# Four PSUM banks as four tiles in the output phase, and a reordered setup, in a fused convolution and GELU feed-forward kernel

## Chip, cores and metric

The kernel runs on one core of one Trainium2 chip. The metric is the device time of one launch in microseconds (us), and the time of a kernel is the median of its runs. The profile is one execution of the same program, taken by the hardware profiler.

## What is computed

A softmax over the 7 taps of 8 heads gives the weights of a causal convolution along the sequence; its result goes through a feed-forward block with the quick GELU. The two weight matrices of that block arrive as float64, and the program rounds them on the chip.

```python
x: (8, 4096, 192)  weight: (8, 7)  w_in: (192, 2048)  w_out: (2048, 192)   # w_in, w_out float64
w = softmax(weight)                       # per head, 24 channels each
c[b, s, d] = sum_k w[head(d), k] * x_pad[b, s + k, d]     # 6 zeros ahead of the sequence
h = c.reshape(32768, 192) @ w_in
g = h * sigmoid(1.702 * h)
out = g @ w_out                           # (32768, 192), float32
```

## The kernel before

The work is cut into 64 steps of 256 positions for each half of the batch. Two neighbouring steps share one load of `x`, one transposition and one convolution: `prepare(big)` yields, for such a pair, three transposes on VectorE (DVE), the load of the next pair, and 21 convolution operations (3 channel groups of 7 taps) that write the tile `ct`. They are spread over the two steps ahead. Each step has two phases on TensorE (PE):

- `hidden(s, u)`, eight times (`u` from 0 to 7): 12 products (float32, so 24 matmul instructions) into a `ph` tile of two banks, out of two that rotate; then ScalarE (ACT) applies the GELU into `g`. A step has 192 matmul instructions of this kind, at line L286.
- `output(s)`: seven products `p1, p6, c11, p7, p5, p3, p4` of a Strassen-Winograd scheme, 96 matmul instructions each (48 at L316 and 48 at L326), into the `po` tile. After each product DVE reads the result out of PSUM: L347 copies it, L350, L355, L358, L360, L362 and L365 add it to a running sum in `u`, and `turn` (L340) transposes a finished quarter into `osb`, which 24 DMAs of the SP queue then write out.

The order of the phases on PE is hidden(0), hidden(1), output(0), hidden(2), output(1), and so on up to hidden(63), output(62), output(63). Between the DVE operations of `output(s-1)` stand the four operations of `sums_g(s)` (L300 to L303), which form the sums of `g` that the products need.

All seven products share one tile of four banks: `p1` and `c11` use bank 0, `p6` and `p3` bank 1, `p7` and `p4` bank 2, `p5` bank 3.

```python
psum_o = ctx.enter_context(tc.tile_pool(name="psum_o", bufs=1, space=bass.MemoryType.PSUM))
po = psum_o.tile([P, NR, TOK], F32, name="po")      # NR = 4 banks
dst = po[:, bank, at : at + TA]
```

Each engine runs its instructions in the order in which the program text emits them; a tile library inserts the waits between engines. In the setup the order is written out by hand: `load_x(0)`, then eight DMAs for four pieces of `w_in` into a scratch area, `prepare(0)` (DVE: transposes and the whole convolution of the first pair), then `round_w_in(0)` (DVE: seven operations over 128x768 and two more over 64x768, then two copies on ACT). hidden(0) follows, with `round_w_in(1)` to `(3)` between its parts and `prepare(1)` spread over steps 0 and 1. After hidden(1) stand `round_w_out(0)` to `(3)` and `sums_w_out`. The scratch area for the raw weights is one of the two buffers of `g`; `g` of step 1 takes the same buffer, so that its first GELU waits until the last `round_w_out` has read it.

Of the kernel before, what the change touches and what calls it, by code (L numbers as in the profile page):

```python
# [8 lines left out]
F32 = mybir.dt.float32  # L9
# [6 lines left out]
def kernel(  # L16
# [56 lines left out]
    u_pool = ctx.enter_context(tc.tile_pool(name="u", bufs=1))  # L73
    osb_pool = ctx.enter_context(tc.tile_pool(name="osb", bufs=2))
    psum_h = ctx.enter_context(tc.tile_pool(name="psum_h", bufs=2, space=bass.MemoryType.PSUM))
    psum_o = ctx.enter_context(tc.tile_pool(name="psum_o", bufs=1, space=bass.MemoryType.PSUM))

    ctx.enter_context(tc.manual_schedule())

# [38 lines left out]

    w8 = consts.tile([H, K], F32)
    nc.scalar.dma_start(out=w8, in_=weight)  # L120
    load_x(0)

    w_in_s = consts.tile([P, NC, F], F32)
    w_in_v = moe_w_in.bitcast(U32).rearrange("(c q) (h f) -> h q c f", q=R, h=2)
    w_out_v = moe_w_out.bitcast(U32).rearrange("(c p) d -> p c d", p=P)

    for i in range(NW):
        piece = raw[:, i, :].rearrange("p (c f) -> p c f", c=NC)  # L130
        cols = slice(2 * i * FW, 2 * (i + 1) * FW)
        for h in range(2):
            nc.sync.dma_start(out=piece[halves[h], :, :], in_=w_in_v[h, :, :, cols])

# [22 lines left out]
    def round_piece(i, dsts):  # L157

        words = raw[:, i, :].rearrange("p (n w) -> p n w", w=2)
        lo, hi = words[:, :, 0], words[:, :, 1]  # L160
        m_hi, m_lo, e, m = (tmp[:, j, :] for j in range(4))
        vec = nc.vector

        vec.tensor_scalar(m_hi, hi, 0xFFFFF, 1 << 20, op0=ALU.bitwise_and, op1=ALU.bitwise_or)
# [11 lines left out]
        for rows, c, cols, dst in dsts:  # L176
            vec.scalar_tensor_tensor(
                out=dst,
                in0=m[rows, :].bitcast(F32).rearrange("p (c n) -> p c n", c=c)[:, :, cols],
                scalar=2.0**-20,  # L180
                in1=e[rows, :].bitcast(F32).rearrange("p (c n) -> p c n", c=c)[:, :, cols],
                op0=ALU.mult,
                op1=ALU.mult,
            )

    def round_w_in(i):
        cols = [slice(h * HF + i * FW, h * HF + (i + 1) * FW) for h in range(2)]
        round_piece(
            i, [(halves[h], NC, slice(0, FW), w_in_s[halves[h], :, cols[h]]) for h in range(2)]
        )  # L190
        for h in range(2):
            nc.scalar.copy(w_in_s[halves[1 - h], :, cols[h]], w_in_s[halves[h], :, cols[h]])

    def load_w_out():
        for i in range(NW):
# [5 lines left out]
    def round_w_out(i):  # L201
        k, j = divmod(i * CW, NK)
        round_piece(
            i,
            [
                (slice(0, P), CW, slice(m * HD, (m + 1) * HD), w_out_s[:, 2 * m + k, j : j + CW, :])
                for m in range(2)
            ],
        )
# [17 lines left out]
    NR = 4  # L227
    pw = psum_o.tile([P, NR, TOK], F32, name="po")[:, 0, 0 : NC * K].rearrange(
        "p (c k) -> p c k", c=NC
    )  # L230
    for c in range(NC):
        nc.tensor.matmul(pw[:, c, :], sel[:, c, :], e8, start=True, stop=True)
    cw = consts.tile([P, NC, K], F32)
# [14 lines left out]
        if c == NC - 1:  # L248
            xins.pop(big)

    def conv(big, i):
        c, k = divmod(i, K)
        if i == 0:
            cts[big] = ct_pool.tile([P, NC, TOK], F32, name="ct")
        src = xts[big][:, c, k : k + TOK]
        dst = cts[big][:, c, :]
        tap = cw[:, c, k : k + 1]
        if k == 0:
            nc.vector.tensor_scalar_mul(dst, src, tap)  # L259
        else:  # L260
            nc.vector.scalar_tensor_tensor(  # L261
                out=dst, in0=src, scalar=tap, in1=dst, op0=ALU.mult, op1=ALU.add
            )

    def prepare(big):

        for c in range(NC):
            yield lambda c=c: transpose_x(big, c)
        if big + 1 < N_BIG:
            yield lambda: load_x(big + 1)  # L270
        for i in range(NC * K):
            yield lambda i=i: conv(big, i)

    def hidden(s, u):

        i, k = divmod(u, 2)
        if u == 0:
            gs[s] = new_g()
        ph = psum_h.tile([P, 2, 2, T], F32, name="ph")
        ct = cts[s // 2]  # L280
        t = s % 2 * T
        for j in range(2):
            f = k * HF + (2 * i + j) * P
            for c in range(NC):
                for h in range(2):
                    nc.tensor.matmul(  # L286
                        ph[:, h, j, :],
                        w_in_s[halves[h], c, f : f + P],
                        ct[halves[h], c, t : t + T],
                        start=(c == 0),  # L290
                        stop=(c == NC - 1),
                    )
        nc.scalar.activation(  # L293
            gs[s][:, 2 * k : 2 * k + 2, 2 * i : 2 * i + 2, :], ph, AF.Gelu_apprx_sigmoid
        )

    def sums_g(s):

        g = [gs[s][:, i, :, :] for i in range(NS)]
        yield nc.vector.tensor_sub(g[T1], g[B12], g[B11])  # L300
        yield nc.vector.tensor_sub(g[T3], g[B22], g[B12])  # L301
        yield nc.vector.tensor_sub(g[T2], g[B22], g[T1])  # L302
        yield nc.vector.tensor_sub(g[T4], g[T2], g[B21])  # L303

    def output(s, others):

        g = gs.pop(s)
        po = psum_o.tile([P, NR, TOK], F32, name="po")
        u = u_pool.tile([P, 4, TA], F32, name="u")
        osb = osb_pool.tile([P, 2, 2, TA], F32, name="osb")  # L310

        def product(a, b, bank, at, first=True):
            dst = po[:, bank, at : at + TA]
            for j in range(NK):
                for c in range(3):
                    nc.tensor.matmul(  # L316
                        dst[c * Q : (c + 1) * Q, :],
                        w_out_s[:, a, j, c * Q : (c + 1) * Q],
                        g[:, b, j, 0:TA],
                        start=(first and j == 0),  # L320
                        stop=(j == NK - 1),
                        skip_group_check=True,
                    )

                for c in range(3):
                    nc.tensor.matmul(  # L326
                        dst[3 * Q :, c * TB : (c + 1) * TB],
                        w_out_s[:, a, j, c * Q : (c + 1) * Q],
                        g[:, b, j, TA:T],
                        start=(first and j == 0 and c == 0),  # L330
                        stop=(j == NK - 1),
                        skip_group_check=True,
                    )
            return dst
# [49 lines left out]
                        ),  # L384
                    )

    for work in prepare(0):
        work()
    round_w_in(0)

    todo = []
    for s in range(N_ST + 1):
        if s < N_ST:
            if s % 2 == 0 and s // 2 + 1 < N_BIG:
                todo = list(prepare(s // 2 + 1))
            n = -(-len(todo) // (2 - s % 2))
            now, todo = todo[:n], todo[n:]
            for u in range(NK):
# [5 lines left out]
                for work in now[u * n // NK : (u + 1) * n // NK]:  # L404
                    work()
            if s == 1:
                for i in range(NW):
                    round_w_out(i)
                sums_w_out()
        others = sums_g(s) if s < N_ST else iter(())  # L410
        if s > 0:
            output(s - 1, others)
        for _ in others:
            pass


# [28 lines left out]
```

## Time and profile before

| | |
|---|---|
| median of 3 runs | 2938.97 us (2938.91 to 2939.54) |
| the profiled execution | 2938.98 us, span 2937.3 us, mean granted clock 0.992 |
| PE busy | 2637.6 us (90% of the span), 55302 matmul instructions |
| DVE busy | 1396.2 us (48%) |
| ACT busy | 533.6 us (18%) |
| POOL (GpSimd) busy | 2.2 us, 11 instructions |
| chain that ended last | PE 89%, DVE 8%, issue 1%, DMA 1% |

Matmuls overlap one another, so a busy PE says that at least one is in flight. What tells more here is the start of the same line in two neighbouring steps, and the rows that name what ended an idle time of PE. Two times of the profile are always given together: when something started, counted from the start of the span, and how long it took.

### The profile page before, as it was taken

What the parts mean: (1) busy time and instruction counts of PE and PEld (TensorE: products, weight loads), DVE (VectorE), ACT (ScalarE), POOL (GpSimd) and SP (SyncE); (2) the same over time, 40 slices, a digit from 0 to 9 for tenths busy, and PEclk for the clock granted to TensorE, in tenths of its full rate; (3) what the DMA queues carried; (4) which work ended last, traced back from release to release, by engine and by line L of the source; (5) the groups of instructions that cost most, each with busy time, mean ns of one, the idle gap of its engine ahead of it and who ended that gap; (6) DMA issues with size and microseconds to landing.
All of it is one profiled execution on the core that took longest, in us unless ns stands there. A gap on an engine that the chain in (4) does not pass through costs nothing.

```text
span 2937.3 us, 115577 instructions
## 1 busy us (share of the span) xinstructions
PE 2637.6 (90%) x55302; PEld 2411.5 (82%) x55302; DVE 1396.2 (48%) x1841; ACT 533.6 (18%) x524; POOL 2.2 (0%) x11
## 2 busy tenths in 40 slices
PE   4599999999999999999999999999999999999997
PEld 3488888888888888888888888888888888888886
DVE  8644445445445444445444444444454454454432
ACT  2121121121121121221211211211211211211210
POOL 0000000000000000000000000000000000000000
PEclk9799999999999999999999999999999999999999
DMA  6011110111110111110111111111101111101000
GB/s 140 3 30 31 27 30 14 27 30 31 28 29 13 28 30 29 30 30 11 29 30 28 29 24 17 30 31 27 29 18 23 30 31 28 30 12 28 12 12 15
DMA packets 293030, 80.90 MB, mean 28 GB/s; under 512 B 223440, under 2 KB 291024, under 8 KB 292560
## 3 DMA queue, kind: packets, MB, share of 16 engines
q1 hardware_dynamic: 292544, 73.51, 14.6%
q8 instruction: 432, 7.08, 1.0%
q14 instruction: 38, 0.31, 0.0%
q10 hardware_dynamic: 16, 0.00, 0.0%
HBM read 48.23 MB, written 25.17 MB: 25 GB/s over the span
## 4 chain that ended last, share of the span: by engine, by line
PE 89%; DVE 8%; issue 1%; DMA 1%; SPq 0%; ACT 0%; ACTq 0%
PE ph L286 46%; PE po L326 26%; PE po L316 18%; DVE osb L340 2%; DVE u L362 1%; DVE u L355 1%; DVE u L358 1%; DVE u L347 1%; DVE u L350 1%; DVE u L360 1%; DMA xin<-in_x_dram 0%; DMA g<-in_moe_w_in_dram 0%; DVE ct L261 0%; ACT g L293 0%; DVE g L173 0%
## 5 line engine op out<-in xcount | busy, mean ns | idle before, releaser
L316 PE MATMUL po<-g,w_out_s 128*32 128x192 f32 x21504 | 1254.8, 328 | 215.9 <-DVE u L360 70.3
L286 PE MATMUL ph<-ct,w_in_s 64*128 64x256 f32 x12288 | 1351.4, 378 | 67.7 <-ACT g L293 35.4
L286 PEld LDWEIGHTS ph<-ct,w_in_s 64*128 64x128 f32 x12288 | 1189.0, 188 | 210.7 <-ACT g L293 35.8
L326 PE MATMUL po<-g,w_out_s 128*32 128x64 f32 x21504 | 1284.6, 220 | 0.0
L326 PEld LDWEIGHTS po<-g,w_out_s 128*32 128x32 f32 x21504 | 1212.2, 110 | 0.0
L316 PEld LDWEIGHTS po<-g,w_out_s 128*32 128x32 f32 x21504 | 834.7, 109 | 299.0 <-DVE u L360 80.6
L293 ACT ACTIVATE g<-ph 128x1024 f32<-128x1024 f32 x512 | 524.0, 1024 | 2314.6 <-PE ph L286 2250.5
L300 DVE TENSOR_TENSOR g<-g 128x2048 f32<-128x2048 f32 x64 | 146.7, 2292 | 659.7 <-ACT g L293 659.7
L261 DVE SCALAR_TENSOR_TENSOR ct<-xt,cw,ct 128x512 f32<-128x512 f32 x576 | 431.8, 750 | 19.4
L303 DVE TENSOR_TENSOR g<-g 128x2048 f32<-128x2048 f32 x64 | 146.2, 2285 | 0.0
L302 DVE TENSOR_TENSOR g<-g 128x2048 f32<-128x2048 f32 x64 | 146.2, 2285 | 0.0
L301 DVE TENSOR_TENSOR g<-g 128x2048 f32<-128x2048 f32 x64 | 146.0, 2281 | 0.3 <-ACT g L293 0.3
L362 DVE TENSOR_TENSOR u<-u,po 128x192 f32<-128x192 f32 x64 | 22.7, 355 | 190.7 <-PE po L326 190.7
L355 DVE TENSOR_TENSOR u<-u,po 128x192 f32<-128x192 f32 x64 | 22.6, 354 | 190.8 <-PE po L326 190.8
L365 DVE TENSOR_TENSOR u<-u,po 128x192 f32<-128x192 f32 x64 | 22.7, 354 | 164.3 <-PE po L326 164.3
L347 DVE COPY u<-po 128x192 f32<-128x192 f32 x64 | 22.9, 358 | 131.7 <-PE po L326 131.7
L340 DVE STREAM_TRANSPOSE osb<-u 128x192 f32<-128x192 f32 x192 | 72.6, 378 | 6.6
L244 DVE STREAM_TRANSPOSE xt<-xin 128x512 f32<-128x512 f32 x96 | 60.3, 679 | 3.5 <-DMA xin<-in_x_dram 3.5
L340 DVE STREAM_TRANSPOSE osb<-po 128x192 f32<-128x192 f32 x64 | 24.5, 382 | 52.0 <-PE po L326 49.1
L350 DVE TENSOR_TENSOR u<-u,po 128x192 f32<-128x192 f32 x64 | 22.7, 354 | 52.3 <-PE po L326 52.3
L358 DVE TENSOR_TENSOR u<-u,po 128x192 f32<-128x192 f32 x64 | 22.6, 353 | 52.0 <-PE po L326 52.0
L259 DVE TENSOR_SCALAR ct<-xt,cw 128x512 f32<-128x512 f32 x96 | 45.1, 470 | 0.0
(34 smaller groups left out, 93.1 us busy)
## 6 DMA issues: line engine op xcount, KB each, us to landing
xin<-in_x_dram SPq DMA_DIRECT2D x128, 320.0 KB, 6.2
out_dram<-osb SPq DMA_DIRECT2D x768, 24.0 KB, 1.6
out_dram<-osb SPq DMA_DIRECT2D x768, 8.0 KB, 1.5
g<-in_moe_w_in_dram SPq DMA_DIRECT2D x8, 384.0 KB, 13.2
g<-in_moe_w_out_dram SPq DMA_DIRECT2D x4, 768.0 KB, 11.5
w<-in_weight_dram ACTq DMA_DIRECT2D x1, 0.2 KB
```

The source lines that it names most:

```text
L244: nc.vector.transpose(xts[big][:, c, PAD:].rearrange("p (j t) -> p j t", t=Q), xins[big][:, :, c * R : c * R + Q],)
L261: nc.vector.scalar_tensor_tensor(out=dst, in0=src, scalar=tap, in1=dst, op0=ALU.mult, op1=ALU.add)
L286: nc.tensor.matmul(ph[:, h, j, :], w_in_s[halves[h], c, f : f + P], ct[halves[h], c, t : t + T], start=(c == 0), stop=(c == NC - 1),)
L293: nc.scalar.activation(gs[s][:, 2 * k : 2 * k + 2, 2 * i : 2 * i + 2, :], ph, AF.Gelu_apprx_sigmoid)
L300: yield nc.vector.tensor_sub(g[T1], g[B12], g[B11])
L301: yield nc.vector.tensor_sub(g[T3], g[B22], g[B12])
L302: yield nc.vector.tensor_sub(g[T2], g[B22], g[T1])
L303: yield nc.vector.tensor_sub(g[T4], g[T2], g[B21])
L316: nc.tensor.matmul(dst[c * Q : (c + 1) * Q, :], w_out_s[:, a, j, c * Q : (c + 1) * Q], g[:, b, j, 0:TA], start=(first and j == 0), stop=(j ...
L326: nc.tensor.matmul(dst[3 * Q :, c * TB : (c + 1) * TB], w_out_s[:, a, j, c * Q : (c + 1) * Q], g[:, b, j, TA:T], start=(first and j == 0 a ...
L340: vec.transpose(osb[:, m, n, :].rearrange("p (j d) -> p j d", d=Q), src.rearrange("p (j t) -> p j t", t=Q),)
L347: vec.tensor_copy(u1, p1)
```

## The change

There are four edits. First, the output phase allocates four `po` tiles of one bank each, from a pool of four buffers, in place of one tile of four banks; the products write the same banks in the same order. Second, the setup is emitted in another order: the first piece of `w_in` is loaded ahead of `x` and rounded ahead of `prepare(0)`, the convolution of the first pair is done in two halves of 256 positions, the first ahead of hidden(0) and the second at its end, the rounding of `w_out` is emitted within hidden(1), and `prepare(1)` as a whole after output(0). Third, `w_in_s` has another layout, so that the last operation of a rounding is one over 128 partitions in place of two over 64. Fourth, the sums of `g` of steps 0 and 1 are on GpSimd.

```diff
-    psum_o = ctx.enter_context(tc.tile_pool(name="psum_o", bufs=1, space=bass.MemoryType.PSUM))
+    psum_o = ctx.enter_context(tc.tile_pool(name="psum_o", bufs=4, space=bass.MemoryType.PSUM))
...
-    load_x(0)
-    w_in_s = consts.tile([P, NC, F], F32)
+    w_in_s = consts.tile([P, NC, 2, HF], F32)
...
             nc.sync.dma_start(out=piece[halves[h], :, :], in_=w_in_v[h, :, :, cols])
+        if i == 0:
+            load_x(0)
...
     def round_w_in(i):
-        cols = [slice(h * HF + i * FW, h * HF + (i + 1) * FW) for h in range(2)]
-        round_piece(
-            i, [(halves[h], NC, slice(0, FW), w_in_s[halves[h], :, cols[h]]) for h in range(2)]
-        )
+        cols = slice(i * FW, (i + 1) * FW)
+        round_piece(i, [(NC, slice(0, FW), w_in_s[:, :, 0, cols])])
         for h in range(2):
-            nc.scalar.copy(w_in_s[halves[1 - h], :, cols[h]], w_in_s[halves[h], :, cols[h]])
+            nc.scalar.copy(w_in_s[halves[1 - h], :, 1, cols], w_in_s[halves[h], :, 0, cols])
...
+        parts = [(0, TOK)] if big else [(0, T), (T, TOK)]
+        for t0, t1 in parts:
+            for i in range(NC * K):
+                yield lambda i=i, t0=t0, t1=t1: conv(big, i, t0, t1)
...
     def sums_g(s):
+        eng = nc.gpsimd if s < 2 else nc.vector
-        yield nc.vector.tensor_sub(g[T1], g[B12], g[B11])
+        yield eng.tensor_sub(g[T1], g[B12], g[B11])
...
-        po = psum_o.tile([P, NR, TOK], F32, name="po")
+        banks = [psum_o.tile([P, TOK], F32, name="po") for _ in range(4)]
...
-            dst = po[:, bank, at : at + TA]
+            dst = banks[bank][:, at : at + TA]
...
-    for work in prepare(0):
+    round_w_in(0)
+    todo = list(prepare(0))
+    for work in todo[: -NC * K]:
         work()
-    round_w_in(0)
+    first = todo[-NC * K :]
...
             for u in range(NK):
                 hidden(s, u)
...
                 if s == 0 and u == NK - 1:
                     load_w_out()
+                    for work in first:
+                        work()
+                if s == 1 and u < NW:
+                    round_w_out(u)
+                    if u == NW - 1:
+                        sums_w_out()
...
         if s > 0:
             output(s - 1, others)
         for _ in others:
             pass
+        if s == 1:
+            for work in todo:
+                work()
```

What the change moves is seen best in the order of the instructions on the engines. On PE, in the output phase of step 4, before, at the end of `c11` and the start of `p7` (the number behind `po` tells tiles apart; DVE_49 is the semaphore that DVE counts up):

```order
L316 MATMUL po_2534<-g_1898,w_out_s_101 32x192 x3
L326 MATMUL po_2534<-g_1898,w_out_s_101 32x64 x3
L316 MATMUL po_2534<-g_1898,w_out_s_101 32x192 [waits DVE_49]
L316 MATMUL po_2534<-g_1898,w_out_s_101 32x192 x2
L326 MATMUL po_2534<-g_1898,w_out_s_101 32x64 x3
```

Every one of the seven products starts with such a wait. The same output phase now, from the end of `p6` (po_2564) over `c11` (po_2563), `p7` (po_2565) and `p5` (po_2566) to `p3`:

```order
L327 MATMUL po_2564<-g_1924,w_out_s_101 32x64 x3
L317 MATMUL po_2563<-g_1924,w_out_s_101 32x192 [waits DVE_49]
L317 MATMUL po_2563<-g_1924,w_out_s_101 32x192 x2
L327 MATMUL po_2563<-g_1924,w_out_s_101 32x64 x3
...
L317 MATMUL po_2565<-g_1924,w_out_s_101 32x192 x3
L327 MATMUL po_2565<-g_1924,w_out_s_101 32x64 x3
...
L317 MATMUL po_2566<-g_1924,w_out_s_101 32x192 x3
L327 MATMUL po_2566<-g_1924,w_out_s_101 32x64 x3
...
L317 MATMUL po_2564<-g_1924,w_out_s_101 32x192 [waits DVE_49]
```

`p1`, `p7` and `p5` have lost their wait. `p6`, `c11`, `p3` and `p4` keep one, now for the last reader of their own bank.

On DVE, at the start of the program, before:

```order
L234 COPY cw<-po 128x21
L240 MEMSET xt 128x3x6
L244 STREAM_TRANSPOSE xt<-xin 128x512 x3
L259 TENSOR_SCALAR ct<-xt,cw 128x512
L261 SCALAR_TENSOR_TENSOR ct<-xt,cw,ct 128x512 x6
...
L164 TENSOR_SCALAR g<-g 128x768
...
L173 SCALAR_TENSOR_TENSOR g<-g 128x768
L177 SCALAR_TENSOR_TENSOR w_in_s<-g 64x3x256 x2
```

and now:

```order
L230 COPY cw<-po 128x21
L165 TENSOR_SCALAR g<-g 128x768
...
L174 SCALAR_TENSOR_TENSOR g<-g 128x768
L178 SCALAR_TENSOR_TENSOR w_in_s<-g 128x3x256
L236 MEMSET xt 128x3x6
L240 STREAM_TRANSPOSE xt<-xin 128x512 x3
L255 TENSOR_SCALAR ct<-xt,cw 128x256
L257 SCALAR_TENSOR_TENSOR ct<-xt,cw,ct 128x256 x6
```

The rounding of the first piece of `w_in` has moved ahead of the transposes, and the convolution ahead of hidden(0) covers half as many positions.

On DVE, around output(0), before, from the last of the four sums of `w_out` on:

```order
L216 TENSOR_TENSOR w_out_s<-w_out_s 128x768
L300 TENSOR_TENSOR g<-g 128x2048
L347 COPY u<-po 128x192
L301 TENSOR_TENSOR g<-g 128x2048
L350 TENSOR_TENSOR u<-u,po 128x192
```

and now, from the same place to the convolution of the second pair:

```order
L215 TENSOR_TENSOR w_out_s<-w_out_s 128x768
L348 COPY u<-po 128x192
L351 TENSOR_TENSOR u<-u,po 128x192
...
L366 TENSOR_TENSOR u<-u,po 128x192
L341 STREAM_TRANSPOSE osb<-u 128x192
L238 COPY xt<-xt 128x3x6
L240 STREAM_TRANSPOSE xt<-xin 128x512 x3
L255 TENSOR_SCALAR ct<-xt,cw 128x512
L257 SCALAR_TENSOR_TENSOR ct<-xt,cw,ct 128x512 x6
```

The sums of `g` have left this place for GpSimd, where the eight operations now stand alone, and the transposes and the convolution of the second pair, which DVE did in steps 0 and 1 ahead of the rounding of `w_out`, have come in behind output(0).

More of the change, by code (lines that the diff above doesn't have):

```diff
@@ L175, in round_piece @@
         )
-        for rows, c, cols, dst in dsts:
+        for c, cols, dst in dsts:
             vec.scalar_tensor_tensor(
                 out=dst,
-                in0=m[rows, :].bitcast(F32).rearrange("p (c n) -> p c n", c=c)[:, :, cols],
+                in0=m.bitcast(F32).rearrange("p (c n) -> p c n", c=c)[:, :, cols],
                 scalar=2.0**-20,
-                in1=e[rows, :].bitcast(F32).rearrange("p (c n) -> p c n", c=c)[:, :, cols],
+                in1=e.bitcast(F32).rearrange("p (c n) -> p c n", c=c)[:, :, cols],
                 op0=ALU.mult,
@@ L205, in round_w_out @@
             [
-                (slice(0, P), CW, slice(m * HD, (m + 1) * HD), w_out_s[:, 2 * m + k, j : j + CW, :])
+                (CW, slice(m * HD, (m + 1) * HD), w_out_s[:, 2 * m + k, j : j + CW, :])
                 for m in range(2)
@@ L226 @@
     nc.vector.tensor_scalar_mul(e8, e8, esum)
[L227 to L230, printed above, removed]
+    pw = psum_o.tile([P, TOK], F32, name="po")[:, 0 : NC * K].rearrange("p (c k) -> p c k", c=NC)
     for c in range(NC):
@@ L249, in transpose_x, with conv @@
             xins.pop(big)
-    def conv(big, i):
+    def conv(big, i, t0=0, t1=TOK):
         c, k = divmod(i, K)
-        if i == 0:
+        if i == 0 and t0 == 0:
             cts[big] = ct_pool.tile([P, NC, TOK], F32, name="ct")
-        src = xts[big][:, c, k : k + TOK]
-        dst = cts[big][:, c, :]
+        src = xts[big][:, c, k + t0 : k + t1]
+        dst = cts[big][:, c, t0:t1]
         tap = cw[:, c, k : k + 1]
@@ L270, in prepare @@
             yield lambda: load_x(big + 1)
-        for i in range(NC * K):
-            yield lambda i=i: conv(big, i)
+        parts = [(0, TOK)] if big else [(0, T), (T, TOK)]
+        for t0, t1 in parts:
+            for i in range(NC * K):
+                yield lambda i=i, t0=t0, t1=t1: conv(big, i, t0, t1)
     def hidden(s, u):
@@ L282, in hidden @@
         for j in range(2):
-            f = k * HF + (2 * i + j) * P
+            f = (2 * i + j) * P
             for c in range(NC):
@@ L287, in hidden @@
                         ph[:, h, j, :],
-                        w_in_s[halves[h], c, f : f + P],
+                        w_in_s[halves[h], c, k ^ h, f : f + P],
                         ct[halves[h], c, t : t + T],
@@ L297, in sums_g @@
     def sums_g(s):
+        eng = nc.gpsimd if s < 2 else nc.vector
         g = [gs[s][:, i, :, :] for i in range(NS)]
[L300 to L303, printed above, removed]
+        yield eng.tensor_sub(g[T1], g[B12], g[B11])
+        yield eng.tensor_sub(g[T3], g[B22], g[B12])
+        yield eng.tensor_sub(g[T2], g[B22], g[T1])
+        yield eng.tensor_sub(g[T4], g[T2], g[B21])
     def output(s, others):
         g = gs.pop(s)
-        po = psum_o.tile([P, NR, TOK], F32, name="po")
+        banks = [psum_o.tile([P, TOK], F32, name="po") for _ in range(4)]
         u = u_pool.tile([P, 4, TA], F32, name="u")
@@ L385, in output @@
                     )
-    for work in prepare(0):
+    round_w_in(0)
+    todo = list(prepare(0))
+    for work in todo[: -NC * K]:
         work()
-    round_w_in(0)
-    todo = []
+    first = todo[-NC * K :]
     for s in range(N_ST + 1):
-        if s < N_ST:
-            if s % 2 == 0 and s // 2 + 1 < N_BIG:
-                todo = list(prepare(s // 2 + 1))
+        now = []
+        if s == 1:
+            todo = list(prepare(1))
+        elif s < N_ST:
+            if s % 2 == 0:
+                todo = list(prepare(s // 2 + 1)) if 0 < s < N_ST - 2 else []
             n = -(-len(todo) // (2 - s % 2))
             now, todo = todo[:n], todo[n:]
+        if s < N_ST:
             for u in range(NK):
@@ L403 @@
                     load_w_out()
-                for work in now[u * n // NK : (u + 1) * n // NK]:
+                    for work in first:
[4 more added lines that the diff above has]
+                        sums_w_out()
+                for work in now[u * len(now) // NK : (u + 1) * len(now) // NK]:
                     work()
[L406 to L409, printed above, removed]
         others = sums_g(s) if s < N_ST else iter(())
@@ L414 @@
             pass
+        if s == 1:
+            for work in todo:
+                work()
 _INS = ['x', 'weight', 'moe_w_in', 'moe_w_out']
```

## The prediction, made before the changed kernel ran

> **What bounds the kernel now.** I read the page first, then the chain of work that ended last, then who PE waits for, then PE's own order in time at the ends of the products, and last the setup.
>
> The page's first part, with the busy time of PE:
>
> ```profile
> span 2937.3 us, 115577 instructions
> PE 2637.6 (90%) x55302; PEld 2411.5 (82%) x55302; DVE 1396.2 (48%) x1841; ACT 533.6 (18%) x524; POOL 2.2 (0%) x11
> ```
>
> The chain that ended last, in order of time (start, length), where each step shows its hidden phase as one piece:
>
> ```profile
> 32.68 8.74 PE ph L286 x49
> ...
> 65.37 1.03 ACT g L293
> ...
> 105.93 17.88 PE ph L286 x144
> 147.32 20.92 PE ph L286 x192
> ...
> 2857.51 20.92 PE ph L286 x192
> ```
>
> From 147.32 to 2857.51 there are 61 steps of 44.43 us each, of which the hidden phase takes 20.92 and the output phase 23.51. All before them is setup: output(0) starts at 123.8, where the piece of 105.93 ends. So PE sets the pace, and the 10% in which it is idle are these:
>
> ```profile
> PE po L316 <- DVE u L360: 70.3, 64, 1.1
> PE ph L286 <- ACT g L293: 35.4, 1, 35.4
> PE po L316 <- DVE osb L340: 30.4, 64, 0.5
> PE po L316 <- DVE u L347: 28.8, 64, 0.5
> PE po L316 <- DVE u L362: 28.7, 64, 0.4
> PE po L316 <- DVE u L350: 28.7, 64, 0.4
> PE po L316 <- DVE u L355: 28.6, 64, 0.4
> ```
>
> The rows (total us, times, longest) name a product's start and the DVE instruction that read the product before. Six of the seven products wait in each of 64 steps, together 215.5 us, 3.37 a step. The longest, at L360, is the one behind three DVE operations. The 35.4 is a wait of the setup.
>
> **Edit 1, the four tiles.** At most boundaries the tile awaited is another bank than the one about to be written, and where it is the same (`c11` after the copy of `p1`, `p3` after L350, `p4` after L355) the reader is a product's length or more ahead. What a boundary costs is more than its idle time. PE's rows around three boundaries, and two stretches (length, PE busy; the second counts L326 alone, within one product):
>
> ```profile
> 1510.23 0.39 PE L326 MATMUL po<-g,w_out_s 128*32 128x64 f32 x4
> 1511.09 0.36 PE L316 MATMUL po<-g,w_out_s 128*32 128x192 f32 x3 [0.47 <-DVE osb L340]
> ...
> 1500.31 0.81 PE L286 MATMUL ph<-ct,w_in_s 64*128 64x256 f32 x6
> 1501.06 0.36 PE L316 MATMUL po<-g,w_out_s 128*32 128x192 f32 x3
> ...
> 1524.25 0.39 PE L326 MATMUL po<-g,w_out_s 128*32 128x64 f32 x4
> 1524.56 0.49 PE L286 MATMUL ph<-ct,w_in_s 64*128 64x256 f32 x2
> ...
> 1501.06:1524.56 23.50, 20.13 (x674) 19.07 (x672) 10.63 (x13) 1.02 (x1) 0.00 (x0) 1.00 0.04 8
> 1507.75:1510.43 2.68, 2.68 (x48) 2.68 (x48) 1.00 0.00 0
> ```
>
> With a wait, the last matmul drains to 1510.62 before the next product starts at 1511.09. Without one (hidden to `p1`, `p4` to hidden) the next starts 0.06 to 0.08 before the last ends, and matmuls of one form inside a product overlap by about 0.2. A product keeps its 48 L326 matmuls in flow for 2.68, while its busy time with fill and drain is 20.13/7 = 2.88. So a boundary without a wait gives back the idle time, 3.37 a step, and the overlap, 6 x 0.2 = 1.2. Bounds of the saving: 64 x 3.37 = 216 us if the drains stay, 64 x 4.57 = 292 if none does. I take 291: both boundaries in the trace that have no wait overlap, and the form does not even change here. The output phase becomes 18.95.
>
> Does a new wait arise? DVE keeps its order, and its longest operations between the products are the sums of `g`:
>
> ```profile
> L300 DVE TENSOR_TENSOR g<-g 128x2048 f32<-128x2048 f32 x64 | 146.7, 2292 | 659.7 <-ACT g L293 659.7
> L347 DVE COPY u<-po 128x192 f32<-128x192 f32 x64 | 22.9, 358 | 131.7 <-PE po L326 131.7
> 1525.46 0.32 SPq L376 DMA_DIRECT2D out_dram<-osb  x1
> ...
> 1534.47 0.44 SPq L380 DMA_DIRECT2D out_dram<-osb  x1
> ```
>
> A sum and a read take 2.29 + 0.36 = 2.65 of a product's 2.68, at most one sum stands between two products, and three gaps have none, so DVE stays level. The tightest wait is `c11`'s, for the copy of `p1`: done about 0.6 after `p1`'s last matmul, needed 2.68 after it. The output DMAs of a step, on the SP queue, have room too: the 18 that come last are issued within 9.5 us, of a step's 39.9.
>
> **Edits 2 to 4, the setup.** DVE bounds it, nearly without a gap:
>
> ```profile
> 9.82 1.90 DVE L244 STREAM_TRANSPOSE xt<-xin 128x512 f32<-128x512 f32 x3 [3.50 <-DMA xin<-in_x_dram]
> 26.97 0.55 DVE L164 TENSOR_SCALAR g<-g 128x768 uint32<-128x768 uint32 x1
> 33.64 0.17 DVE L242 COPY xt<-xt 128x18 f32<-128x18 f32 x1
> 82.10 0.56 DVE L164 TENSOR_SCALAR g<-g 128x768 uint32<-128x768 uint32 x1
> 87.75 0.55 DVE L164 TENSOR_SCALAR g<-g 128x768 uint32<-128x768 uint32 x1
> 104.86 1.94 ACT L293 ACTIVATE g<-ph 128x1024 f32<-128x1024 f32 x2 [38.46 <-DVE w_out_s L177]
> L261 DVE SCALAR_TENSOR_TENSOR ct<-xt,cw,ct 128x512 f32<-128x512 f32 x576 | 431.8, 750 | 19.4
> L177 DVE SCALAR_TENSOR_TENSOR w_in_s<-g 64x768 f32<-64x768 f32 x8 | 7.6, 953 | 0.3
> L177 DVE SCALAR_TENSOR_TENSOR w_out_s<-g 128x384 f32<-128x384 f32 x8 | 4.1, 554 | 0.1
> 8.00:10.00 2.00, 0.00 (x0) 0.00 (x0) 0.18 (x1) 0.00 (x0) 0.00 (x0) 1.00 1.12 214
> ```
>
> Rounding a piece of `w_in` takes 33.64 - 26.97 = 6.67, now one operation of 0.95 less, 5.7; a piece of `w_out` 87.75 - 82.10 = 5.65. Transposes and convolution of a pair take 26.97 - 9.82 = 17.15, so the convolution 15.3. A half costs more than half of it: the L177 rows give 399 ns for 384 elements, so a tap of 256 is 750 - 266 = 484 ns, and with the gaps a half is about 10.5 (estimate). On SP, the 0.79 MB piece of `w_in` goes ahead of `x` (214 GB/s in the last row): 3.7 us, so `x` lands near 14 instead of 9.8. The first rounding runs in that wait. Then, on DVE: transposes to 16, half a convolution to 26.4 (PE starts; before 32.68), three roundings to 43.5, the other half to 54, four roundings of `w_out` to 76.6. There the GELU of step 1 is released, before at 104.8, and output(0) follows 19 later as now: at 95.6 instead of 123.8. That is 28 us earlier. The loads of `w_out` stand on SP behind those of `x` for the second pair, whose buffer the transposes free at 16; the last of them goes out when the third rounding has freed its piece, near 44. ACT ended `g` of step 0 34 us after PE's start (32.68 to 66.4) and will do so near 60. Neither is last.
>
> What left that stretch comes back. `prepare(1)` now stands on DVE behind the last transpose of output(0), and hidden(2) reads its `ct`. PE is through with output(0) at 114.5; DVE needs 0.8 more for `p4`, then 17.15, to 132.5. PE, stopped for 18, can do the two first channel groups of the first 12 products in between (0.9) and restarts cold: the row of 105.93, after 35 us of idleness, has 17.88 for 144 matmuls, where 20.92/192 each would be 15.7. Net 18 - 0.9 + 2.2 = 19 us lost. Its cover was the setup that DVE bounded; now nothing covers it.
>
> The sums of step 0 (4 x 2.29 on DVE) run on POOL beside the rounding of `w_out`. No row shows such an operation there; the nearest are these:
>
> ```profile
> L147 POOL TENSOR_SCALAR_AFFINE_SELECT sel<-sel 8x128 f32<-8x128 f32 x6 | 1.6, 283 | 0.3
> L143 POOL MEMSET sel<- 8x384 f32 x1 | 0.4, 408 | 0.3 <-POOLq L429 0.3
> L429 POOL MEMSET const-float32-0.0<- 128x1 f32 x1 | 0.1, 103 | 0.3 <-issue 0.3
> ```
>
> The memsets give 0.8 ns an element without an input, the select 1.4 with one, so 2.0 with two: 4.3 us an operation, 17 for four (estimate). They start near 58 and end near 77 to 80, ahead of `p6` at 98; those of step 1 run beside output(0) and end ahead of output(1) near 154. In both cases they are hidden. [...]
>
> Whether DVE slows meanwhile no row shows either: 0 us if the two don't meet, 17 if DVE stands still as long as POOL works. I take 9, as if they shared: both only move data through SBUF, DVE's 2.29 for 2048 elements is 1.1 ns each for two inputs, about POOL's rate for one.
>
> **Sum**: -291 (boundaries) - 28 (setup) + 19 (hidden(2)) + 9 (POOL) = -291. The profiled execution took 2938.98, 1.7 over its span and equal to the median of 2938.97. Forecast: 2648 us.
>
> **Rivals.**
> 1. POOL and DVE exclude each other: DVE loses all 17, so 2656. That DVE works nearly without a pause then, with two inputs in most operations, speaks for it. [...] Chance 0.23.
> 2. They don't meet: 2639. For it: POOL's work is off the path as long as DVE wins. Chance 0.20.
> 3. The waits go, the drains stay: 216 in place of 291, so 2723; or a boundary overlaps only by 0.08, as those between two forms do: 64 x (3.37 + 0.5) = 248, so 2691. Against it: matmuls inside a product overlap more. Chance 0.12.
> 4. The waits turn into issue time. PE issues 674 + 672 instructions in 23.50, 57 per us; without gaps 1344 in 18.95, 71 per us. If 57 is what its supply holds, the output phase stays at 23.5 and only the setup's terms are left: 2939, no change. Against it: 2.68 for 96 matmuls and 96 loads is 72 per us, though for 2.7 us only. Chance 0.02.
> 5. Slower than before: PE without pauses is granted a lower clock. A step of 39.87 us at full clock reaches 44.43 when the clock falls under 0.90, and every step from the setup on is then longer. Against it: the window of 23.50 above has clock 1.00, and PE is at work for 20.13 of it. [...] Chance 0.03.
>
> **How the numbers follow.** Forecast 0.40, rivals as given. The forecast and rivals 1 and 2 lie within 2639 to 2656; the setup's estimates add about 10 on either side, and the range reaches up to rival 3's smaller case: 2628 to 2691. About 0.2% (6 us) is what a measurement can tell from no change. Faster has all but rivals 4 and 5: 0.95; the same 0.02; slower 0.03.
>
> **What would show it.** The period of the hidden phases tells edit 1: 39.9 us if right, 41.0 if the drains stay, 44.4 if the waits come back; PE's waits for DVE in the output phase should be gone from the 64-fold rows. Output(0) should start at 96 to 105: the earlier, the less POOL disturbed DVE, which the durations of L165 to L178 then show. PE should have one wait of 17 to 18 us for `ct` ahead of hidden(2), ended by L257. What would make the forecast wrong is above all a product boundary that costs more than the trace shows, since its price counts 384 times.

## The result, and the profile after

The changed kernel takes 2653.21 us (median of 4 runs, 2652.01 to 2654.05), against 2938.94 (2938.62 to 2939.54) for the kernel before on the same chip: a ratio of 0.9027, with an interval of 0.9012 to 0.9043. The forecast was 2648, the range 2628 to 2691. The profiled execution took 2653.25, 2.1 over its span.

The first lines of the page of the changed kernel, and two of its rows of groups:

```profile
span 2651.2 us, 115606 instructions
PE 2563.9 (97%) x55302; PEld 2394.8 (90%) x55302; DVE 1395.8 (53%) x1850; ACT 533.5 (20%) x524; POOL 39.2 (1%) x19
L317 PE MATMUL po<-g,w_out_s 128*32 128x192 f32 x21504 | 1205.1, 330 | 0.1
L301 DVE TENSOR_TENSOR g<-g 128x2048 f32<-128x2048 f32 x62 | 142.2, 2293 | 645.8 <-ACT g L292 645.8
```

PE is now busy for 97% of the span instead of 90%. In the row of L317 (L316 before), which starts every product, the last number is its idle time: 0.1 us in the whole run. The sums of `g` on DVE are 62 of each kind in place of 64, and as long as before. All rows of PE's waits:

```profile
PE ph L285 <- DVE ct L257: 33.1, 6, 13.2
PE ph L285 <- ACT g L292: 32.3, 1, 32.3
PE ph L285 <- ACT w_in_s L191: 5.5, 3, 2.0
PE po L228 <- DVE e L225: 4.6, 1, 4.6
PE po L327 <- issue: 0.4, 2, 0.2
```

The six rows with 64 waits each are gone, and none took their place. What is left belongs to the setup, but for the last row, which the section on the hardware takes up. The first row is new: six waits for the convolution at L257, of which three (17.5) stand at the start of hidden(0), where L177 was awaited before, and three at hidden(2). The chain that ended last, in order of time (start, length):

```profile
93.48 17.69 PE ph L285 x144
...
148.12 22.00 PE ph L285 x184
189.02 20.92 PE ph L285 x192
229.29 20.92 PE ph L285 x192
269.11 20.92 PE ph L285 x192
308.93 20.92 PE ph L285 x192
```

Most steps last 39.82 us (269.11 to 308.93) in place of 44.43: the hidden phase is still 20.92, the output phase 18.90 instead of 23.51. The step from 189.02 to 229.29 is 0.45 longer; the section on the hardware comes back to it. Output(0) starts at 111.1 (93.48 + 17.69), 12.6 earlier than before, and ahead of the piece of 148.12 stands the new wait. All together, in us of span: 64 x (18.898 - 23.508) = -295.0, the start of output(0) -12.6, the wait at hidden(2) +19.1, pauses of PE +2.2: -286.3. The spans differ by 286.1.

### The profile page after: what moved, and what is told of

Same layout as the page of the kernel before. It is cut to its first block, busy times and chain, and to the rows that moved or that the text cites. A ratio compares the mean times of both kernels' runs of the same rounds, so it can differ in the third digit from the quotient of the medians.

```text
span 2651.2 us, 115606 instructions
## 1 busy us (share of the span) xinstructions
PE 2563.9 (97%) x55302; PEld 2394.8 (90%) x55302; DVE 1395.8 (53%) x1850; ACT 533.5 (20%) x524; POOL 39.2 (1%) x19
## 4 chain that ended last, share of the span: by engine, by line
PE 95%; DVE 3%; DMA 0%; issue 0%; SPq 0%; ACT 0%; DVEq 0%; ACTq 0%
PE ph L285 50%; PE po L327 29%; PE po L317 17%; DVE ct L257 1%; DVE g L174 0%; DMA xin<-in_x_dram 0%; DVE g L172 0%; DVE g L173 0%; DVE g L171 0%; DVE g L167 0%; DVE w_out_s L178 0%; DVE xt L240 0%; DVE g L165 0%; DVE g L166 0%; DVE ct L255 0%
## 5 line engine op out<-in xcount | busy, mean ns | idle before, releaser
L327 PE MATMUL po<-g,w_out_s 128*32 128x64 f32 x21504 | 1214.5, 219 | 0.4 <-issue 0.4
L317 PE MATMUL po<-g,w_out_s 128*32 128x192 f32 x21504 | 1205.1, 330 | 0.1
L327 PEld LDWEIGHTS po<-g,w_out_s 128*32 128x32 f32 x21504 | 1202.7, 110 | 1.0 <-issue 1.0
L317 PEld LDWEIGHTS po<-g,w_out_s 128*32 128x32 f32 x21504 | 625.4, 108 | 22.5 <-issue 22.2
L301 DVE TENSOR_TENSOR g<-g 128x2048 f32<-128x2048 f32 x62 | 142.2, 2293 | 645.8 <-ACT g L292 645.8
L257 DVE SCALAR_TENSOR_TENSOR ct<-xt,cw,ct 128x512 f32<-128x512 f32 (+1 forms) x594 | 435.7, 734 | 20.0
L304 DVE TENSOR_TENSOR g<-g 128x2048 f32<-128x2048 f32 x62 | 141.6, 2284 | 0.0
L303 DVE TENSOR_TENSOR g<-g 128x2048 f32<-128x2048 f32 x62 | 141.6, 2284 | 0.0
L302 DVE TENSOR_TENSOR g<-g 128x2048 f32<-128x2048 f32 x62 | 141.5, 2282 | 0.1
L356 DVE TENSOR_TENSOR u<-u,po 128x192 f32<-128x192 f32 x64 | 22.7, 354 | 147.6 <-PE po L327 147.6
L348 DVE COPY u<-po 128x192 f32<-128x192 f32 x64 | 22.9, 358 | 146.7 <-PE po L327 146.7
L366 DVE TENSOR_TENSOR u<-u,po 128x192 f32<-128x192 f32 x64 | 22.7, 354 | 122.8 <-PE po L327 122.8
L363 DVE TENSOR_TENSOR u<-u,po 128x192 f32<-128x192 f32 x64 | 22.7, 354 | 108.6 <-PE po L327 108.6
L341 DVE STREAM_TRANSPOSE osb<-u 128x192 f32<-128x192 f32 x192 | 72.6, 378 | 6.6
L255 DVE TENSOR_SCALAR ct<-xt,cw 128x512 f32<-128x512 f32 (+1 forms) x99 | 45.7, 462 | 0.0
L341 DVE STREAM_TRANSPOSE osb<-po 128x192 f32<-128x192 f32 x64 | 24.5, 383 | 12.3 <-PE po L327 2.3
L359 DVE TENSOR_TENSOR u<-u,po 128x192 f32<-128x192 f32 x64 | 22.7, 354 | 13.2 <-PE po L327 6.0
L351 DVE TENSOR_TENSOR u<-u,po 128x192 f32<-128x192 f32 x64 | 22.7, 354 | 12.2 <-PE po L327 4.6
```

The lines of the kernel that those rows point to most:

```text
L257: nc.vector.scalar_tensor_tensor(out=dst, in0=src, scalar=tap, in1=dst, op0=ALU.mult, op1=ALU.add)
L301: yield eng.tensor_sub(g[T1], g[B12], g[B11])
L302: yield eng.tensor_sub(g[T3], g[B22], g[B12])
L303: yield eng.tensor_sub(g[T2], g[B22], g[T1])
L304: yield eng.tensor_sub(g[T4], g[T2], g[B21])
L317: nc.tensor.matmul(dst[c * Q : (c + 1) * Q, :], w_out_s[:, a, j, c * Q : (c + 1) * Q], g[:, b, j, 0:TA], start=(first and j == 0), stop=(j ...
```

## The experiments

Each was timed in turns with the kernel before. Where two spans are compared, they are those of the profiled executions, taken apart in the same way: the start of output(0); what output(0) and hidden(2) last beyond 18.90 (or the usual length of that kernel) and 20.92; the usual output phase; and what single output phases last beyond it ("pauses").

**The four tiles without the rest.** The kernel before, with the first edit only:

```diff
-    psum_o = ctx.enter_context(tc.tile_pool(name="psum_o", bufs=1, space=bass.MemoryType.PSUM))
+    psum_o = ctx.enter_context(tc.tile_pool(name="psum_o", bufs=4, space=bass.MemoryType.PSUM))
...
-        po = psum_o.tile([P, NR, TOK], F32, name="po")
+        banks = [psum_o.tile([P, TOK], F32, name="po") for _ in range(4)]
...
-            dst = po[:, bank, at : at + TA]
+            dst = banks[bank][:, at : at + TA]
```

> The kernel before with the four tiles alone, its setup untouched. If the boundaries are all of the gain and the reordered setup is a small loss: 64 steps of 39.82 us in place of 44.43, 2939 - 292 = 2647 us, below the changed kernel's 2653. Rival: part of the gain comes from the reordered setup; then this kernel lies above 2653, by as much as that part.

It took 2652.72 us (2646.41 to 2655.14), ratio 0.9026 (0.9013 to 0.904). The output phase is 18.898 as in the changed kernel, so the tiles alone bring the 295, and the whole gain. Expected were 2647: the median is 5.7 above that, and with runs that lie 8.7 us apart it does not tell whether this kernel is faster or slower than the changed one; the last experiment asks that again. The waits of PE:

```profile
PE ph L283 <- ACT g L290: 35.4, 1, 35.4
PE po L323 <- issue: 0.9, 4, 0.2
```

The first is the setup's wait of before (L286, L293 there), unchanged. The second is new and shows a part of the pauses of PE. By the lengths of the output phases they add up to 4.4 us in this execution (span 2644.7), the shortest of its runs; another one (span 2652.1, the last experiment) has 8.3.

**The setup without the tiles.** The changed kernel with the first edit reversed.

> The changed kernel with the one tile of four banks back. If the edits add up: output(0) starts 12.6 us earlier than before, hidden(2) waits 19 us longer, and every step is 44.43 again: 2939 + 6.5 = 2945 us. Rival, the reordered setup is a gain of its own: below 2939.

It took 2947.05 us (2946.6 to 2947.55), ratio 1.0032 (1.002 to 1.0043). All six waits are back; two of them:

```profile
PE po L317 <- DVE u L361: 70.3, 64, 1.1
PE po L317 <- DVE osb L341: 30.4, 64, 0.5
```

Output(0) starts at 112.7, 11.0 earlier than before, and the wait at hidden(2) costs 8.2 + 11.1 = 19.2. The reordered setup by itself thus adds 8 us: edits 2 to 4 lose more at hidden(2) than they gain ahead of output(0).

**Two tiles of two banks.** This asks whether a wait really hangs on the tile, and not on the bank. With banks 0 and 1 in one tile and 2 and 3 in the other, three products should find their tile read long before, and three should not.

```diff
-    psum_o = ctx.enter_context(tc.tile_pool(name="psum_o", bufs=4, space=bass.MemoryType.PSUM))
+    psum_o = ctx.enter_context(tc.tile_pool(name="psum_o", bufs=2, space=bass.MemoryType.PSUM))
...
-        banks = [psum_o.tile([P, TOK], F32, name="po") for _ in range(4)]
+        pairs = [psum_o.tile([P, 2, TOK], F32, name="po") for _ in range(2)]
...
-            dst = banks[bank][:, at : at + TA]
+            dst = pairs[bank // 2][:, bank % 2, at : at + TA]
```

> The changed kernel with two tiles of two banks each (banks 0 and 1, banks 2 and 3). If a product waits for the last read of the tile that it writes, counted by the tile: p6 (after the read of p1), c11 (after p6) and p5 (after p7) wait as before the change, p7, p3 and p4 find their tile long read. Three boundaries at 3.34 in place of 2.68 us a step: 64 x 3 x 0.66 = 126 us more, 2779 us. If waits went by bank, or the gain came from something else than the tiles: 2653 us. If any sharing brings all the waits back: 2945 us.

It took 2777.7 us (2777.0 to 2778.35), ratio 0.9454 (0.9438 to 0.947). These are the waits of PE that occur in every step:

```profile
PE po L317 <- DVE u L348: 29.1, 64, 0.5
PE po L317 <- DVE u L351: 28.6, 64, 0.4
PE po L317 <- DVE u L356: 28.5, 64, 0.4
```

They stand at `p6`, `c11` and `p5`, each of which follows a product in the same tile. The output phase is 20.86. Three waits fewer shorten it by 2.65, of which idle time is (70.3 + 30.4 + 28.7)/64 = 2.02 (the rows of L360, L340 and L362 before), so 0.63 is overlap won at three boundaries, 0.2 each. The same 0.2 follows from the changed kernel: 23.51 - 18.90 = 4.61 at six boundaries, 3.37 of it idle time.

**The sums of `g` on DVE.** The changed kernel without its fourth edit: `eng = nc.vector`.

> The changed kernel with the sums of g of steps 0 and 1 back on DVE. If GpSimd and DVE exclude each other, DVE gets 16.9 us back in the rounding of w_out and pays about 9.2 for the sums and 2 for waiting until g of step 0 is complete: output(0) starts some 6 us earlier, 2647 us. If the long DVE operations beside GpSimd had another cause and the move relieves DVE: some 9 us later, 2662 us.

It took 2651.88 us (2649.97 to 2652.79), ratio 0.9026 (0.9012 to 0.9039). Output(0) starts where this piece of hidden(1) ends (93.48 and 17.69 in the changed kernel):

```profile
87.34 18.55 PE ph L285 x144
```

That is at 105.8, 5.3 earlier than in the changed kernel, about as a full exclusion has it: putting the four sums on GpSimd cost more than leaving them where they were. The time did not follow, since this profiled execution lost 7.6 us in pauses where the changed kernel lost 2.2. By its total time alone this run tells nothing; the place of output(0) in the trace does.

**`prepare(1)` ahead of output(0).** The work that PE waits for at hidden(2) moves into the time in which PE runs hidden(1); the sums stay on GpSimd.

```diff
                     if u == NW - 1:
                         sums_w_out()
+                        for work in todo:
+                            work()
...
-        if s == 1:
-            for work in todo:
-                work()
```

> The changed kernel with the transposes and the convolution of the second pair (prepare(1)) emitted on DVE right behind the sums of w_out, ahead of output(0). In the changed kernel DVE stands idle there for 17.9 us (96.2 to 114.0). If the 19 us that PE loses ahead of hidden(2) come from the order on DVE alone, they go: 2653 - 19 = 2634 us; up to 5 us of it may come back, since GpSimd's sums of step 1 start at 109.7 and can hold up the end of the convolution and with it the read of p1. If the second pair's x or another load is what hidden(2) waits for: 2653 us.

It took 2651.17 us (2648.38 to 2653.45), ratio 0.9022 (0.9009 to 0.9036), and so missed what was expected. Hidden(2) waits for nothing any more, but output(0) takes 34.93 us. DVE and POOL there, in the timeline:

```profile
108.33 0.48 DVE L255 TENSOR_SCALAR ct<-xt,cw 128x512 f32<-128x512 f32 x1
108.84 21.33 DVE L257 SCALAR_TENSOR_TENSOR ct<-xt,cw,ct 128x512 f32<-128x512 f32 x6
130.09 0.35 DVE L348 COPY u<-po 128x192 f32<-128x192 f32 x1
...
109.55 4.56 POOL L301 TENSOR_TENSOR g<-g 128x2048 f32<-128x2048 f32 x1 [35.90 <-ACT g L292]
...
124.02 4.82 POOL L304 TENSOR_TENSOR g<-g 128x2048 f32<-128x2048 f32 x1
```

Six operations of the convolution take 21.33, which elsewhere take 4.69 (143.38 in the timeline further down): 16.6 lost beside the four sums of step 1 on GpSimd, where up to 5 had been allowed. Behind them on DVE stands the copy of `p1` at L348, for which the next products queue:

```profile
PE po L317 <- DVE u L348: 14.0, 1, 14.0
```

The stall was not removed but moved, from hidden(2) to output(0). It is the exclusion a second time, with other operations.

**GpSimd after DVE.** Here a copy of one column of the last `w_out` sum, on GpSimd, holds the sums back until DVE is through with the weights; nothing else on GpSimd or DVE changes.

```diff
                     if u == NW - 1:
                         sums_w_out()
+                        hold = consts.tile([P, 1], F32)
+                        nc.gpsimd.tensor_copy(hold, w_out_s[:, S4, NK - 1, HD - 1 : HD])
+                        for _ in sums_g(0):
+                            pass
...
-        others = sums_g(s) if s < N_ST else iter(())
+        others = sums_g(s) if 0 < s < N_ST else iter(())
```

> The changed kernel in which GpSimd first reads one column of the last sum of w_out and so starts the sums of step 0 only when DVE is through with w_out. Nothing else moves. If exclusion is what the move to GpSimd costs, and costs only where DVE has work of its own: rounding undisturbed, output(0) starts 16.9 us earlier, 2636 us. If GpSimd's time itself is on the path (T2 for p6 is then done about 14 us behind the sums of w_out, near 93): some us more. If the long DVE operations have another cause: 2653 us.

It took 2640.67 us (2638.26 to 2642.6), ratio 0.8986 (0.8971 to 0.9001). The first sum of step 0, and the piece of hidden(1) at whose end output(0) starts:

```profile
78.68 4.52 POOL L301 TENSOR_TENSOR g<-g 128x2048 f32<-128x2048 f32 x1
...
75.79 17.39 PE ph L285 x144
```

Output(0) starts at 93.1, 18.0 earlier than in the changed kernel, with the same sums on the same engines. Of that, 0.8 us is from `x`, which landed earlier in this execution (the transposes start at 13.12 instead of 13.94); the rest is what it cost that the two engines met. The sums of step 1 end later here and now meet the copy that opens `prepare(1)`:

```profile
110.71 4.51 POOL L304 TENSOR_TENSOR g<-g 128x2048 f32<-128x2048 f32 x1
...
113.03 2.22 DVE L238 COPY xt<-xt 128x18 f32<-128x18 f32 x1
115.17 1.88 DVE L240 STREAM_TRANSPOSE xt<-xin 128x512 f32<-128x512 f32 x3
```

The copy takes 0.13 to 0.17 elsewhere. It ends with the GpSimd operation (115.2), and the wait at hidden(2) is 21.8 instead of 19.1. That and the pauses, 6.1 us in this execution instead of 2.2, are why the time is 4.7 above the expected 2636.

**Everything on DVE, and `prepare(1)` divided.** This puts the two lessons together: no sums on GpSimd; those of step 0 behind the rounding; the transposes and 9 of the 21 operations of the convolution ahead of output(0), the rest between the reads of output(0), where DVE idles; the sums of step 1 behind them.

```diff
-        eng = nc.gpsimd if s < 2 else nc.vector
+        eng = nc.vector
...
+    def rest():
+        left = todo[13:]
+        for n in (0, 2, 5, 5):
+            for work in left[:n]:
+                work()
+            left = left[n:]
+            yield
...
                         sums_w_out()
+                        for _ in sums_g(0):
+                            pass
+                        for work in todo[:13]:
+                            work()
...
-        others = sums_g(s) if s < N_ST else iter(())
+        others = sums_g(s) if 1 < s < N_ST else rest() if s == 1 else iter(())
...
-            for work in todo:
-                work()
+            for _ in sums_g(1):
+                pass
```

> The changed kernel with all sums of g on DVE, those of step 0 behind the sums of w_out, then the transposes and 9 of 21 convolution operations of the second pair, the other 12 between the reads of output(0), and the sums of step 1 behind output(0). If exclusion (16.9 us) and the place of prepare(1) (19.1 us) are the two losses of the reordered setup and nothing else is late next: output(0) starts at 94 in place of 111, hidden(2) waits for nothing, 2653 - 36 = 2617 us. If ACT or a load bounds the setup next: between 2617 and 2634 us. This is also the candidate for the fastest version.

It took 2620.88 us (2620.31 to 2622.39), ratio 0.892 (0.8907 to 0.8934): the fastest of all. Its longest waits, and the piece of hidden(1) at whose end output(0) starts:

```profile
PE ph L285 <- DVE ct L257: 17.9, 3, 13.6
PE ph L285 <- ACT g L292: 15.8, 1, 15.8
...
76.99 18.85 PE L285 MATMUL ph<-ct,w_in_s 64*128 64x256 f32 x144 [15.84 <-ACT g L292]
```

The wait for the GELU of step 1, which the rounding of `w_out` on DVE holds back, fell from 32.3 to 15.8, and the convolution is awaited only in hidden(0). Output(0) starts at 95.8 and takes 18.90, hidden(2) follows without a stall; against the changed kernel that is -15.3 - 19.1, and with 1.6 more of pauses -32.8. The spans differ by 32.6.

**The changed kernel and the tiles alone, once more.** Both on one chip, to see whether the reordered setup is worth anything with the tiles.

> The changed kernel once more, on the same chip and in the same rounds as the kernel with the four tiles alone, since that one's runs spread over 8.7 us (2646.4 to 2655.1) and hide what the reordered setup is worth. If the setup is a loss of 6.5 us, as the profiles' terms give (19.1 lost ahead of hidden(2), 12.6 won before output(0)): 2653 against 2647. If the spread comes from short issue pauses of PE late in the output phases, they hit both alike and each kernel's runs lie 2 to 8 us above the sum of its terms.

> The kernel before with the four tiles alone, beside the changed kernel. If the reordered setup costs 6.5 us: 2647, below the changed kernel by 6. If the two lie within 2 us of each other, the setup is worth nothing either way.

The changed kernel took 2656.49 us (2654.56 to 2657.63, 5 runs), ratio 0.9042 (0.9029 to 0.9054); the tiles alone 2650.88 (2648.84 to 2653.8, 4 runs), ratio 0.9023 (0.901 to 0.9035). The medians differ by 5.6 in the direction and about of the size expected, and no run of the one lies within the runs of the other, though the two intervals overlap, and the changed kernel's first median was 2653.21. With the +0.32% of the setup without the tiles, and with the two terms that the traces show (19.1 lost, 12.6 won), the reordering as it was done is a small loss.

## Why the prediction was right, and which term was not

- **Edit 1**: -291 was forecast; the output phases became 295.0 shorter, of which the pauses take 2.2 back. That boundaries without a wait overlap, against the lower bound of 216, is shown by the two tiles as well: 0.2 a boundary, as taken. The pauses are the small form of rival 4: PE issues 71 instructions per us (1344 in 18.90 us), but not through a whole phase in every step: the one from 209.94 lasts 19.35 (see the section on the hardware).
- **The mis-sized term is POOL beside DVE**: 9 was taken, "as if they shared". It was 16.9, and rival 1 (17, 2656 us) held for this term. In the total, too, rival 1 is nearer (2.8 us) than the forecast (5.2). The timeline of the changed kernel, DVE and POOL together, ahead of output(0):

```profile
54.59 4.61 POOL L301 TENSOR_TENSOR g<-g 128x2048 f32<-128x2048 f32 x1 [51.48 <-ACT g L292]
...
54.74 4.88 DVE L171 TENSOR_SCALAR g<-g 128x768 uint32<-128x768 uint32 x1
59.65 4.74 DVE L172 TENSOR_SCALAR g<-g 128x768 uint32<-128x768 uint32 x1
64.42 4.73 DVE L173 TENSOR_SCALAR g<-g 128x768 uint32<-128x768 uint32 x1
69.19 5.13 DVE L174 SCALAR_TENSOR_TENSOR g<-g 128x768 uint32<-128x768 uint32 x1
74.36 1.03 DVE L178 SCALAR_TENSOR_TENSOR w_out_s<-g 128x384 f32<-128x384 f32 x2
...
77.23 0.55 DVE L171 TENSOR_SCALAR g<-g 128x768 uint32<-128x768 uint32 x1
...
80.00 1.03 DVE L178 SCALAR_TENSOR_TENSOR w_out_s<-g 128x384 f32<-128x384 f32 x2
```

  L171 to L174 take from 54.74 to 74.36, 19.62 us, for the first quarter of `w_out`; for the second, without POOL, from 77.23 to 80.00, 2.77. So 16.85 is lost. One DVE operation goes through for each of POOL's, and lasts about as long as it (4.73 to 5.13 us beside 4.61 to 4.80). This had been given 0.23. One reason named for it does not hold: of the nine DVE operations of a rounding only four have two inputs (L167, L174 and the two of L178), and L171 to L173, with one, were held up (L173: 4.73 us in place of 0.56) as L174, with two, was (5.13 in place of 0.96). By what mechanism the two engines take turns, no row shows.
- **The setup without that**: -28 was forecast, and it is -12.6 - 16.9 = -29.5. Half a convolution took 10.1 (estimate 10.5). The sign "output(0) at 96 to 105" failed by the contention alone: without it, output(0) would start at 111.1 - 16.85 = 94.3.
- **hidden(2)**: +19 was forecast, +19.1 measured, at the place and by the instruction named, but as three waits (7.9, 3.8 and 3.9 us, with the matmuls that PE could do in between), where the signs given ahead have one of 17 to 18. This is in the timeline of DVE:

```profile
130.11 0.35 DVE L366 TENSOR_TENSOR u<-u,po 128x192 f32<-128x192 f32 x1 [1.91 <-PE po L327]
...
143.38 4.69 DVE L257 SCALAR_TENSOR_TENSOR ct<-xt,cw,ct 128x512 f32<-128x512 f32 x6
147.98 0.17 DVE L238 COPY xt<-xt 128x18 f32<-128x18 f32 x1
```

  `prepare(1)` follows the last read of output(0) and ends at 148.0, and at 148.12 PE goes on.
- **Edit 4's price on GpSimd**: 4.3 us an operation was estimated, 4.55 to 4.80 measured.
- **The sum**: the 7.9 that the contention was short, less 1.5 for the setup and 1.8 for the boundaries with their pauses, and 0.4 more outside the span, is 5.0 of the 5.2 us between 2648 and 2653.2.

## What to carry to other kernels

The waits for a buffer followed the tile that was allocated here, not the bank that is written (with two tiles of two banks, 28.5 to 29.1 us in 64 waits each at `p6`, `c11` and `p5`, and none at the other four products): count, for each product, how far back its tile was last read, and make tiles so small that this is a product's length. A wait that counts in every step is priced with the drain and refill around it, here 0.2 us on top of 0.56. Work moved from VectorE to GpSimd was no help here while VectorE was busy on SBUF data: it cost 16.9 us to move 9.2 us of work, and leaving it on VectorE while filling that engine's idle gaps gave the fastest version, 2620.88 us.

## What was not expected of the hardware

**Which DVE operations were held up beside GpSimd.** Beside GpSimd's sums, operations over SBUF with one input (L171, 0.55 to 4.88) and with two (L174, 0.96 to 5.13; L257, 0.75 to about 4.9, with the 16.6 lost in four operations) and a copy of 18 elements (0.17 to 2.22) were stopped. Those that read PSUM (L348, L351, L356, L359, L361, L363; 0.32 to 0.36), and the transposition at L341 (0.38, as at 130.50, behind the last sum), were not. This is the timeline of output(0) in the changed kernel, while GpSimd works from 109.74 to 128.14:

```profile
118.90 4.58 POOL L303 TENSOR_TENSOR g<-g 128x2048 f32<-128x2048 f32 x1
123.56 4.58 POOL L304 TENSOR_TENSOR g<-g 128x2048 f32<-128x2048 f32 x1
...
122.07 0.35 DVE L356 TENSOR_TENSOR u<-u,po 128x192 f32<-128x192 f32 x1 [2.30 <-PE po L327]
124.75 0.35 DVE L359 TENSOR_TENSOR u<-u,po 128x192 f32<-128x192 f32 x1 [2.33 <-PE po L327]
125.14 0.38 DVE L341 STREAM_TRANSPOSE osb<-u 128x192 f32<-128x192 f32 x1
```

L356 and L359 last as long as without GpSimd (the 0.35 of L366 above), and GpSimd itself (4.55 to 4.58) no longer than where DVE was idle (4.51 to 4.57 for the sums of step 0 in the run with GpSimd after DVE). So the sums of step 1 were free where they stood, and those of step 0 were not.

**PE paused for 0.1 to 0.5 us late in some output phases, where most took 18.90.** Two output phases of the changed kernel (length; PE busy, PEld busy), and the weight loads at the place where the first of them stops:

```profile
209.94:229.29 19.35, 19.28 (x674) 18.88 (x674) 10.63 (x13) 1.03 (x1) 0.00 (x0) 1.00 0.06 9
250.21:269.11 18.90, 18.90 (x675) 18.81 (x674) 10.57 (x13) 1.02 (x1) 0.00 (x0) 1.00 0.05 10
...
224.49 0.17 PEld L327 LDWEIGHTS po<-g,w_out_s 128*32 128x32 f32 x2
225.02 0.11 PEld L317 LDWEIGHTS po<-g,w_out_s 128*32 128x32 f32 x1 [0.36 <-issue]
...
q8 instruction: 432, 7.08, 1.1%
```

The clock is full (1.00) in both, and no semaphore ended the 0.36. Such pauses (0.1 to 0.5 us) occur only from 8.4 us after the start of an output phase on, up to its end, and not in the same phases in every execution. They added up, beyond the usual output phase, to 0.03 us in the kernel before and 0.2 in the setup without the tiles (1344 instructions in 23.5 us, 57 per us), 0.4 with two tiles (64 per us), and 2.2 to 8.3 in the profiled executions with 18.9 (71 per us).

The traces also hold the time of each packet of the instruction queue. The queue's row has 432 packets of 16.4 KB; 55302 matmuls and as many weight loads over 432 packets are 256 instructions a packet (estimate). In the eight traces with output phases of 18.9 us (their first and their last two left out), all pauses of a trace stand at the same count of matmuls behind a packet, so that those of one phase are 128 matmuls and 128 loads apart, and each of the 149 ends 1.2 to 1.6 us after a packet has come in. In the phase shown, the packet of 222.17 took 1.37 us, and PE goes on at 225.01, 1.47 after it; the next, of 226.05, took 1.23, and after a second pause PE goes on at 228.74, 1.46 after it. In no phase does the matmul at that count start under 1.2 us after its packet, and where it starts more than 1.65 us after it, no pause stands before it. That PE waits for its instructions there is the author's reading of these times; no run changed their supply, so it was not shown by experiment, and what sets its pace stays open.

The kernels with 18.9 us output phases spread over 2 to 9 us from run to run, where the kernel before spreads over 1 to 3. That the pauses are a large part of it is an estimate from one pair: the two profiled executions of the tiles alone are 7.4 us apart, of which 2.5 lie ahead of output(0) (it starts at 121.9 and 124.4) and the rest in the output phases.
